# Spreading a weight conversion over more steps, and putting off three blocks instead of two

## The chip, the core and the metric

The kernel runs on one core of one Trainium2 chip. The metric is device time in microseconds (us): the median of three runs before the change is 971.77 us (971.24 to 972.63). TensorE is PE in the rows (its weight loads PEld), VectorE is DVE, ScalarE is ACT, GpSimd is POOL, and SyncE is SP, which issues every DMA of this kernel.

## What is computed

Three stages follow each other over 4608 tokens of 512 numbers, all in float32:

```
phi(x) = [exp(p - m), exp(-(p - m))],  p = x @ w_phi,  m = max|p|       # 128 + 128 features of each head
attn   = phi(q) @ (phi(k)^T v) / (phi(q) @ sum phi(k) + 1e-6)            # 8 batches, 8 heads, 576 x 64
x      = attn as (4608, 512)
g      = leaky(x @ w_in; alpha)                                          # d_ff = 2048
y      = g @ w_out                                                       # (4608, 512)
logits = y @ phi;  d = softmax over tokens;  c = softmax over 32 slots
s      = d^T @ y;  slot_out[e] = relu(s[e] @ w1[e]) @ w2[e]              # 8 experts, 4 slots each
out    = c @ slot_out
```

`w_in`, `w_out` and `alpha` arrive as 64-bit floats. The kernel never forms `y`: it uses `phi` folded into `w_out` (`wpr`, 2048 x 32) for the logits and gathers `d^T @ g` first.

## The kernel before

**Blocks and steps.** The tokens go in 12 blocks of 384 (`NB`), and each block in 16 chunks of 128 of d_ff (`NC`): 192 steps. A step computes one chunk of `h = x @ w_in` in `gemm` (L513): 12 matrix products of 128x128 by 128x384 into one of two PSUM banks `ph`, since x and w_in are each split in a high and a low part. `leaky` (L525) empties the bank, ACT first (L527), DVE second (L528), into one of five `gT` tiles. A product can start when L528 of the step two before it has run.

**The four chunks of a quad.** `turn_g` (L545) transposes each `gT` on DVE (L547) into a half of a large tile and, after every fourth, adds four products `pl` (L556) to the block's logits. When a block is complete, `softmax` (L565) copies `pl` to `ls` on ACT (L570), forms `pr` on PE (L575), takes its maximum on DVE (L586), the exponential on ACT (L598), transposes it (L608), and `gather` (L616) adds `d^T g` in 48 products of 32x512 over four banks `pS` (L625) if both halves lie in one tile, or 96 of 32x256 if they don't. DVE then adds the four banks to `acc` (L644). `gather` takes both banks of the pool `ps_a` and the pair of `ps_b`.

**Blocks put off.** The tile `gb` that takes the transposes lies where the pool `prep` lay, and `prep` holds what the conversions of the weights need. So blocks 0 to `NDEF`-1 have their `gT` written to DRAM (`gT_d`, L531) and taken up again later, four steps of `QUADS` for a block: `reload` (L533) loads a quad into three double tiles of the ring `vg` (L537) and the tiles `kp1` and `ks` (L543). Their logits `pl` sit in a bank of `ps_a` from the first quad to `ls`; those of the other blocks have a bank of their own. Their halves are `half_of` (L501): `held` in `kall`, which the K pairs use until step 141, and thirds of `gb`.

**Conversion.** `conv` (L183) turns 64-bit words of one chunk of a weight into float32 in six DVE and three ACT instructions (L197 to L209); for `w_out` a transposition (L236), a product with `phi` (L243) and a gather (L249, with the copy L250 on DVE) follow, three steps long. `prep` is closed at step 16 `NDEF`, and the first transposition into `gb` waits for the last of these.

**Beside the steps.** Attention runs for one block ahead: the 32 K pairs (L257 to L381), and per block four `q_pair` (L385) and a `q_finish` (L457), which sends the reciprocal through DRAM (`rc_d`, `bc`), divides (L486) and splits x into `xhi` (ACT, L479) and `xlo` (DVE, L480). From step 158 on, weights of the last stage are fetched (L716, DMA L733), first `w_out` as float32 (`wo`). `combine` (L689) does the softmax over the slots, its largest part behind step 173. All these functions are put into steps by the table at L668 to L709; within the dependences a list scheduler then fixes the order of each engine, and every engine and SP's DMA issue run strictly in that order. Banks and tiles of a pool are given out as the scheduler comes to them.

Of the kernel before, what the change touches and what calls it, by code (L numbers as in the profile page):

```python
# [11 lines left out]
I32 = mybir.dt.int32  # L12
# [22 lines left out]
VT = 5  # L35
KVB = 8
PF = 14
NDEF = 2
QUADS = [[148, 150, 152, 154], [164, 166, 168, 170]]
EARLY = 4  # L40
KPB = 3
QB = 2
# [19 lines left out]
def attention_prelu_softmoe(ctx: ExitStack, tc, qT, kT, v, wphi, w_in, w_out, alpha, phi, w1, w2, out):  # L62
# [9 lines left out]
    wo32 = dram.tile([NC, 128, DM], F32, name="wo32")  # L72
    gT_d = dram.tile([NDEF, NC, 128, BT], F32, name="gT_d")
    rc_d = [dram.tile([2, 32, 2, HB], F32, name=f"rc_d{i}") for i in range(2)]
# [10 lines left out]
    def close_pool(name):  # L85
        pools.pop(name)[0].__exit__(None, None, None)
# [26 lines left out]
    def bank(name, pool=None):  # L113
        if pool is not None:
            return pool.tile([128, 512], F32, tag={id(ps_h): "h", id(ps_l): "l", id(ps_d): "d"}[id(pool)], name=name)
        taken["a"].append([])
        return ps_a.tile([128, 512], F32, tag="a", name=name)
# [59 lines left out]
    def at(slot, phase, fn):  # L177
        at_step(slot, phase, fn)
# [4 lines left out]
    def conv(slot, src, use):  # L183
        st = {}

        def load():
            st["raw"] = prep.tile([128, 1024], I32, tag="raw", name="raw", bufs=3)
            nc.sync.dma_start(st["raw"], src)

        def first():  # L190
            pair = st["raw"].rearrange("p (n t) -> p n t", t=2)
            st["low"], high = pair[:, :, 0].bitcast(U32), pair[:, :, 1].bitcast(F32)
            m = st["m"] = prep.tile([128, 512], F32, tag="m", name="m", bufs=2)
            sign = st["sign"] = prep.tile([128, 512], F32, tag="sign", name="sign", bufs=2)
            rest = st["rest"] = prep.tile([128, 512], F32, tag="rest", name="rest")
            mu, ru = m.bitcast(U32), rest.bitcast(U32)
            nc.scalar.activation(m, high, AF.Abs)  # L197
            nc.scalar.activation(sign, high, AF.Sign)
            nc.vector.tensor_scalar(out=m, in0=m, scalar1=F64_LEAST, scalar2=F64_MOST, op0=ALU.max, op1=ALU.min)
            nc.vector.tensor_scalar(out=mu, in0=mu, scalar1=3, scalar2=0x40000000, op0=ALU.logical_shift_left, op1=ALU.bitwise_xor)  # L200
            nc.vector.tensor_scalar(out=ru, in0=mu, scalar1=0x7F800000, scalar2=None, op0=ALU.bitwise_and)
            nc.vector.scalar_tensor_tensor(out=rest, in0=st["low"], scalar=2.0 ** -52, in1=rest, op0=ALU.mult, op1=ALU.mult)  # L202
            nc.scalar.activation(m, m, AF.Abs)

        def second():
            m = st["m"]
            nc.vector.tensor_tensor(out=m, in0=m, in1=st["rest"], op=ALU.add)  # L207
            w = prep.tile([128, 512], F32, tag="w32", name="w32", bufs=2)
            mark[slot + 1] = nc.vector.tensor_tensor(out=w, in0=m, in1=st["sign"], op=ALU.mult).ins  # L209
            use(slot, w)  # L210

        at(slot - 2, "pre", load)
        at(slot, "pre", first)
        at(slot + 1, "pre", second)
# [12 lines left out]
    def use_w_out(c):  # L227
        def use(slot, w):
            st = {}
            for i in range(4):  # L230
                nc.sync.dma_start(wo32[4 * i + c // 4, 32 * (c % 4):32 * (c % 4) + 32, :], w[32 * i:32 * i + 32])

            def trans():
                pt = bank("pwt")
                for k in range(KD):
                    nc.tensor.transpose(pt[:, 128 * k:128 * k + 128], w[:, 128 * k:128 * k + 128], ident)  # L236
                st["wT"] = prep.tile([128, 512], F32, tag="wT", name="wT")
                nc.scalar.copy(st["wT"], pt)

            def product():  # L240
                pw = bank("pw", ps_l)
                for k in range(KD):
                    nc.tensor.matmul(pw[32 * k:32 * k + 32, 0:128], phi_sb[:, k, :], st["wT"][:, 128 * k:128 * k + 128], start=True, stop=True)  # L243
                st["sw"] = prep.tile([128, 128], F32, tag="sw", name="sw")
                nc.scalar.copy(st["sw"], pw[:, 0:128])

            def gather():
                pw = bank("pw2", ps_l)
                nc.tensor.matmul(pw[:, 0:32], st["sw"], tident[:, 0:32], start=True, stop=True)  # L249
                nc.vector.tensor_copy(wpr[:, c, :], pw[:, 0:32])  # L250

            at(slot + 2, "pe", trans)
            at(slot + 3, "pe", product)
            at(slot + 4, "pe", gather)
        return use
# [241 lines left out]
    pl_t, pl_read, gT_t = {}, {}, {}  # L497
    odd_turn = {n: n % 2 for n in range(NDEF, NB)}
    held = kall[:, 0:6144].rearrange("p (h c t) -> p h c t", h=2, c=8)

    def half_of(n, h):  # L501
        if n == 0 or (n < NDEF and h):
            return held[:, h]
        return gbt[0][:, 1 if h else 2 if n < NDEF else 2 * odd_turn[n]]

    def turned(n):
        if n == 0:
            return [(held, slice(0, 2))]
        if n < NDEF:
            return [(gbt[0], slice(2, 3)), (held, slice(1, 2))]  # L510
        return [(gbt[0], slice(2, 0, -1) if odd_turn[n] else slice(0, 2))]

    def gemm(n, c):  # L513
        xhi, xlo = xhi_t[n], xlo_t[n]
        ph = ps_h.tile([128, 512], F32, tag="h", name="ph")
        h = ph[:, 0:BT]
        first = [(k, a, b) for k in range(KD) for a, b in ((0, 0), (1, 0))] + [(k, 0, 1) for k in range(KD)]
        terms = first if c == 0 else [(k, a, b) for k in range(KD) for a, b in ((0, 0), (0, 1), (1, 0))]
        for i, (k, a, b) in enumerate(terms):
            gemm_last[0] = nc.tensor.matmul(  # L520
                h, (w_in_hi, w_in_lo)[a][c][:, 128 * k:128 * k + 128], (xhi, xlo)[b][:, k, :],
                start=(i == 0), stop=(i == len(terms) - 1)).ins
        return h

    def leaky(n, c, h):  # L525
# [3 lines left out]
        mark[NC * n + c] = ins  # L529
        if n < NDEF:  # L530
            nc.sync.dma_start(gT_d[n, c], gT)  # L531
# [145 lines left out]
        q_finish(-39 + 18 + 5 if n == 0 else NC * (n - 1) + 7, n)  # L677
    for c in range(NC):
        conv(int(-16 + 1.25 * c), w_in[c].bitcast(I32), use_w_in)
        conv(int(10 + 1.25 * c), w_out[c].bitcast(I32), use_w_out(c))  # L680
    for n in range(NDEF, NB):
        softmax(NC * (n + 1) + 1, n)
    for m, slots in enumerate(QUADS):
        for quad, slot in enumerate(slots):
# [51 lines left out]
    gbt, views = [], []  # L736
# [11 lines left out]
    for step in range(-45, nslots + 4):  # L748
        slot = real.get(step)
        for fn in sched.get((step, "pre"), ()):  # L750
            fn()
        h = None
        if slot is not None:
            n, c = divmod(slot, NC)
            if 0 <= slot < nslots:
                h = gemm(n, c)
            pn, pc = divmod(slot - 1, NC)
            if NDEF <= pn < NB:
                turn_g(pn, pc)
        for fn in sched.get((step, "pe"), []) + sched.get((step, "pe2"), []):  # L760
            fn()
        if h is not None:
            leaky(n, c, h)
        for fn in sched.get((step, "post"), ()):
            fn()
        if slot is None:
            continue
        if slot == NC * NDEF:
            close_pool("prep")
            gbt.append(open_pool("gp").tile([128, 3, 8, BT], F32, tag="gb", name="gb"))  # L770
        if slot == QUADS[0][-1] + 4:
            fetch_k(0, 6)
        if slot == QUADS[1][-1] + 4:
            fetch_k(6, 16)
            fetch(attk, "kp1")
            fetch(attk, "ks")
        if slot == 168:
            close_pool("attq")
            pf = open_pool("pf", "right")
            for i in range(2):  # L780
                fetch(pf, f"hr{i}", 2)
            for i in range(PF - 4):
                fetch(pf, f"pf{i}")
        if slot == NC * (NB - 1):
            fetch(xp, "num", 3)
            fetch(xp, "bc", 3)
        if NC * (NB - 1) < slot <= nslots:
            fetch(wring, f"w{(slot - 1) % NC}", 2)
        if slot == 181:
            fetch_half(0)  # L790
        if slot == nslots:
            fetch(xp, "xhi", 3)
            fetch(xp, "xlo", 3)
# [174 lines left out]
```

## Time and profile before

| | us |
|---|---|
| median of three runs | 971.77 |
| profiled execution, its own time | 973.75 |
| its span, first to last instruction | 971.9 |
| PE busy | 928.3 |
| DVE busy | 722.1 |
| ACT busy | 443.6 |

The profiled execution is 1.85 us longer than its span and 1.98 us longer than the median. Shares over the whole span hide that the stages differ: in the first quarter DVE is nearly always busy, in the middle PE has no idle time at all, and in the last 30 us the DMA engines write the output.

### The profile page before, as it was taken

Reading aid. Unit: us, or ns where it says so; the run is one execution under the profiler, and the core shown is the slowest. Engines: PE = TensorE matmul, PEld = TensorE weight load, DVE = VectorE, ACT = ScalarE, POOL = GpSimd, SP = SyncE. Lnnn points to the kernel's source line nnn. Section 1 sums busy time; section 2 is a strip of 40 time slices with the busy share of each in tenths; the row PEclk is TensorE's granted clock in tenths of the full one; section 3 lists DMA queues with packets and bytes.
Section 4 is the critical chain, followed back from the end, with each engine's and each line's share of the span. In section 5 each row is a group of like instructions: output and inputs, shape, how many; then the busy total and the mean of one; then the engine's idle time right before and its main releaser. Section 6 shows DMA issues by size and latency. Waiting matters only on the chain.

```text
span 971.9 us, 20072 instructions
## 1 busy us (share of the span) xinstructions
PE 928.3 (96%) x8178; PEld 654.1 (67%) x8178; DVE 722.1 (74%) x1425; ACT 443.6 (46%) x867; POOL 143.5 (15%) x84
## 2 busy tenths in 40 slices
PE   6888989999989999999999999999999999899997
PEld 3446676777668676676677776776777667786454
DVE  6998999989686687677677778677756767864233
ACT  5876757766635345245335344353342341221113
POOL 4102212112112112122022112121130220000000
PEclk9898999999999999999999999999999999999999
DMA  7345655674231031031211210200212609478999
GB/s 272 119 141 177 207 169 196 213 203 122 64 87 28 23 85 43 26 78 53 51 44 42 59 53 25 75 26 23 54 34 72 177 1 302 159 268 260 311 354 335
DMA packets 75675, 122.22 MB, mean 126 GB/s; under 512 B 7872, under 2 KB 49472, under 8 KB 75584
## 3 DMA queue, kind: packets, MB, share of 16 engines
q1 hardware_dynamic: 75584, 120.95, 40.3%
q8 instruction: 64, 1.05, 0.5%
q14 instruction: 27, 0.22, 0.1%
HBM read 99.82 MB, written 21.10 MB: 124 GB/s over the span
## 4 chain that ended last, share of the span: by engine, by line
PE 74%; DVE 17%; DMA 4%; issue 2%; ACT 2%; SPq 0%; DVEq 0%; ACTq 0%
PE ph L520 37%; PE num L440 5%; PE pkv L336 5%; PE pS L625 4%; PE pl L556 4%; PE pq L407 3%; PE den L445 3%; PE pk L293 2%; PE pso L866 2%; DVE m L207 2%; DVE gT L528 1%; PE pe L846 1%; DVE mx L281 1%; PE po L902 1%; DVE rest L202 1%
## 5 line engine op out<-in xcount | busy, mean ns | idle before, releaser
L520 PE MATMUL ph<-xhi,w 128*128 128x384 f32 x1536 | 430.8, 351 | 8.2 <-ACT xhi L479 4.0
L520 PEld LDWEIGHTS ph<-xhi,w 128*128 128x128 f32 x1536 | 280.3, 189 | 71.5 <-issue 38.0
L520 PE MATMUL ph<-xlo,w 128*128 128x384 f32 x768 | 257.9, 341 | 0.9 <-DVE xlo L480 0.8
L419 POOL PARTITION_ALL_REDUCE mb<-pj x48 | 137.4, 2864 | 477.4 <-ACT pj L413 326.8
L527 ACT ACTIVATE gT<-ph 128x384 f32<-128x384 f32 x192 | 93.3, 488 | 245.3 <-PE ph L520 239.9
L528 DVE SCALAR_TENSOR_TENSOR gT<-gT,alpha_rest,ph 128x384 f32<-128x384 f32 x192 | 115.7, 604 | 103.8 <-ACT gT L527 102.4
L520 PEld LDWEIGHTS ph<-xlo,w 128*128 128x128 f32 x768 | 144.4, 189 | 9.7 <-issue 4.8
L547 DVE STREAM_TRANSPOSE gb<-gT 128x384 f32<-128x384 f32 x162 | 92.0, 571 | 2.9
L429 ACT ACTIVATE qe<-pj 128x768 f32<-128x768 f32 x90 | 72.2, 839 | 22.9 <-DVE pj L423 14.0
L440 PE MATMUL num<-qe,kv 128*64 128x192 f32 (+1 forms) x488 | 68.6, 411 | 3.5 <-ACT qe L429 3.3
L336 PE MATMUL pkv<-kall 128*64 128x256 f32 x464 | 57.9, 393 | 1.3 <-ACT kall L287 0.7
L281 DVE TENSOR_REDUCE mx<-pk 128x4 f32<-128x512 f32 (+1 forms) x80 | 49.5, 623 | 7.2 <-PE pk L293 5.8
L407 PE MATMUL pq<-qraw,wp 64*128 64x384 f32 x192 | 46.8, 545 | 7.9 <-DMA qraw<-in_qT_dram 4.1
L286 ACT ACTIVATE kall<-kall 128x512 f32<-128x512 f32 x60 | 37.5, 627 | 30.4 <-DVE kall L283 30.2
L440 PEld LDWEIGHTS num<-qe,kv 128*64 128x64 f32 x488 | 31.1, 136 | 27.8 <-issue 18.0
L324 DVE TENSOR_TENSOR ks<-ks,kall 128x256 f32<-128x256 f32 x96 | 47.4, 517 | 0.4
L336 PEld LDWEIGHTS pkv<-kall 128*64 128x64 f32 x464 | 31.6, 140 | 23.5 <-issue 4.8
L423 DVE TENSOR_TENSOR pj<-pj,mb 128x768 f32<-128x768 f32 x48 | 44.8, 932 | 0.0
L283 DVE TENSOR_TENSOR kall<-pk,mx 128x512 f32<-128x512 f32 x60 | 40.8, 680 | 2.2 <-PE pkv L336 1.7
L293 PE MATMUL pk<-wp,kall 64*128 64x128 f32 x512 | 39.5, 293 | 2.9 <-issue 2.6
L293 PEld LDWEIGHTS pk<-wp,kall 64*128 64x128 f32 x512 | 32.9, 194 | 12.8 <-issue 10.8
L413 ACT COPY pj<-pq 128x768 f32<-128x768 f32 x44 | 35.0, 796 | 13.4 <-PE pq L407 13.2
(203 smaller groups left out, 1157.6 us busy)
## 6 DMA issues: line engine op xcount, KB each, us to landing
w<-in_w_dram SPq DMA_DIRECT2D x46, 256.0 KB
kall<-in_v_dram SPq DMA_DIRECT2D x30, 320.0 KB
qraw<-in_qT_dram SPq DMA_DIRECT2D x48, 192.0 KB
bc<-rc_d SPq DMA_DIRECT2D x24, 384.0 KB
out_dram<-os SPq DMA_DIRECT2D x18, 512.0 KB
raw<-in_w_in_dram SPq DMA_DIRECT2D x16, 512.0 KB
raw<-in_w_out_dram SPq DMA_DIRECT2D x16, 512.0 KB
gT_d<-gT SPq DMA_DIRECT2D x32, 192.0 KB
```

The lines of the kernel that those rows point to most:

```text
L281: nc.vector.tensor_reduce(out=mx[:, 0:nt], in_=src, axis=AX.X, op=ALU.max, apply_absolute_value=True)
L293: lambda t=t, j=j, sl=slice(64 * j, 64 * j + 64): nc.tensor.matmul(st["pk"][:, j, F * t:F * t + F], st["kraw"][sl, 128 * t:128 * t + 128], ...
L324: nc.vector.tensor_tensor(out=ks[:, j], in0=ks[:, j], in1=f[t], op=ALU.add)
L336: return lambda: nc.tensor.matmul(pkv[64 * j:64 * j + 64, 0:256], st["vt"][:, t, 64 * j:64 * j + 64], part.rearrange("p s f -> p (s f)"), ...
L407: lambda j=j, sl=slice(64 * j, 64 * j + 64): nc.tensor.matmul(pq[j][:, 0:BT], wp[sl, F * j:F * j + F], st["qraw"][sl], start=True, stop=True)
L419: nc.gpsimd.partition_all_reduce(mb, pj, 128, bass_isa.ReduceOp.absmax)
L429: nc.scalar.activation(st["e", s], pj, AF.Exp, scale=(1.0, -1.0)[s])
L440: lambda s=s, j=j: nc.tensor.matmul(num[64 * j:64 * j + 64, o:o + w], kvs[:, s, 64 * j:64 * j + 64], st["e", s][:, j, o:o + w], start=(s = ...
L520: gemm_last[0] = nc.tensor.matmul(h, (w_in_hi, w_in_lo)[a][c][:, 128 * k:128 * k + 128], (xhi, xlo)[b][:, k, :], start=(i == 0), stop=(i = ...
L527: nc.scalar.activation(gT, h, AF.Relu, scale=-1.0)
L528: ins = nc.vector.scalar_tensor_tensor(out=gT, in0=gT, scalar=alpha_rest[:, c:c + 1], in1=h, op0=ALU.mult, op1=ALU.add).ins
L547: nc.vector.transpose(out=half_of(n, c // 8)[:, c % 8, :], in_=gT)
```

## The change

`NDEF` goes from 2 to 3, so that block 2 too is written to DRAM and `prep` stays open until step 48. The conversions of `w_out` start at steps 10 + 2.2 c (10 to 43) instead of 10 + 1.25 c (10 to 28). The blocks put off are taken up in three groups, at steps 146 to 152, 156 to 162 and 166 to 172, instead of two at 148 to 154 and 164 to 170. Block 1 now has both halves in `held`; blocks 0 and 2 have one in `held` and one in `gb`, so the gathers of two blocks instead of one take 96 products. The first fetch of `wo` into `held` moves from step 158 to 166, the second from 174 to 176.

```diff
-NDEF = 2
-QUADS = [[148, 150, 152, 154], [164, 166, 168, 170]]
+NDEF = 3
+QUADS = [[146, 148, 150, 152], [156, 158, 160, 162], [166, 168, 170, 172]]
...
     def half_of(n, h):
-        if n == 0 or (n < NDEF and h):
+        if n == 1:
             return held[:, h]
-        return gbt[0][:, 1 if h else 2 if n < NDEF else 2 * odd_turn[n]]
+        if n < NDEF:
+            return gbt[0][:, n] if h else held[:, n // 2]
+        return gbt[0][:, 1 if h else 2 * odd_turn[n]]
 
     def turned(n):
-        if n == 0:
+        if n == 1:
             return [(held, slice(0, 2))]
         if n < NDEF:
-            return [(gbt[0], slice(2, 3)), (held, slice(1, 2))]
+            return [(held, slice(n // 2, n // 2 + 1)), (gbt[0], slice(n, n + 1))]
...
-        conv(int(10 + 1.25 * c), w_out[c].bitcast(I32), use_w_out(c))
+        conv(int(10 + 2.2 * c), w_out[c].bitcast(I32), use_w_out(c))
...
-        if slot == QUADS[0][-1] + 4:
+        if slot == QUADS[1][-1] + 4:
             fetch_k(0, 6)
-        if slot == QUADS[1][-1] + 4:
+        if slot == QUADS[2][-1] + 4:
             fetch_k(6, 16)
```

Lines from L503 on have numbers two higher after the change (L520 is L522, L625 is L627).

**First place: PE, at the last chunk of `w_out`.** `pw` is the gather of a chunk, `pkv`, `den` and `num` are attention, `w_850` is chunk 7 of block 2 before, `w_615` chunk 0 of block 3 after. Before:

```order
L445 MATMUL den<-qe,zt 32x192 x4
L249 MATMUL pw_2892<-tident,sw 128x32
L336 MATMUL pkv<-kall 64x256 x8
L336 MATMUL pkv<-kp,kall 64x256 x2
L556 MATMUL pl<-gT,wpr 32x384 x4
L342 MATMUL pkv<-ks,ones 32x128 x4
L520 MATMUL ph<-xhi,w_850 128x384
```

After:

```order
L522 MATMUL ph<-xhi,w_1226 128x384
L293 MATMUL pk<-wp,kall 128x128 x8
L249 MATMUL pw_3439<-tident,sw 128x32
L440 MATMUL num<-qe,kv 64x192 x8
L522 MATMUL ph<-xhi,w_615 128x384 x6
L445 MATMUL den<-qe,zt 32x192 x8
```

Before, 36 rows of attention and conversion stand between the products of steps 38 and 39, and the last gather of `w_out` is among them; now that gather stands between the products of steps 47 and 48, which follow each other.

**Second place: PE, the last block put off.** `pr` belongs to block 1 before and to block 2 now, `pS` is its gather; `w_1061` and `w_1226` are steps 172 and 175, `w_615` is step 176. Before:

```order
L575 MATMUL pr<-ls,tident 128x384
L520 MATMUL ph<-xhi,w_1024 128x384
...
L520 MATMUL ph<-xhi,w_1061 128x384
L625 MATMUL pS<-gb,d 32x256 x48
L625 MATMUL pS<-kall,d 32x256 x48
L556 MATMUL pl<-gT,wpr 32x384 x4
```

After:

```order
L522 MATMUL ph<-xhi,w_1226 128x384
L577 MATMUL pr<-ls,tident 128x384
L627 MATMUL pS<-kall,d 32x256 x48
L627 MATMUL pS<-gb,d 32x256 x48
L522 MATMUL ph<-xhi,w_615 128x384 x8
```

Before, the products of steps 171 and 172 stand between `pr` and its gather; now nothing does.

**Third place: DVE, the same stretch after the change,** from the leaky step 173 (first row) to that of step 174 (last row):

```order
L530 SCALAR_TENSOR_TENSOR gT<-gT,alpha_rest,ph 128x384
L486 TENSOR_TENSOR num<-bc,num 128x384 x4
L549 STREAM_TRANSPOSE gb<-gT_8505 128x384
L480 TENSOR_TENSOR xlo<-num,xhi 128x384
L588 TENSOR_REDUCE mbl<-pr 128x1
L610 STREAM_TRANSPOSE d<-dT 128x384
...
L695 TENSOR_REDUCE cm<-logits 128x28
L696 TENSOR_TENSOR logits<-logits,cm 128x896
L698 TENSOR_REDUCE cm<-logits 128x28
L704 TENSOR_TENSOR cw<-logits,cm 128x512
L530 SCALAR_TENSOR_TENSOR gT<-gT,alpha_rest,ph 128x384
```

The division, transpositions of the block put off (`gT_8505` is one that was reloaded), its softmax and the whole first part of `combine` now stand between two leaky steps; before, three leaky steps (171 to 173) stood between the maximum of `pr` and the division, and the division came behind `combine`, not ahead of it.

## Rows read from the trace of the kernel before

**Rows 1.** The page, parts 1 and 2: busy us, share; tenths per fortieth.

```profile
PE 928.3 (96%) x8178; PEld 654.1 (67%) x8178; DVE 722.1 (74%) x1425; ACT 443.6 (46%) x867; POOL 143.5 (15%) x84
...
PE   6888989999989999999999999999999999899997
...
DVE  6998999989686687677677778677756767864233
```

**Rows 2.** Windows: from:to, length, busy us (count) by engine, PE clock, DMA, GB/s.

```profile
145.00:285.00 140.00, 134.58 (x1087) 98.23 (x1085) 124.88 (x253) 89.53 (x177) 22.35 (x12) 0.99 0.51 153
185.00:205.00 20.00, 19.94 (x151) 15.60 (x150) 17.48 (x38) 14.38 (x30) 0.21 (x1) 1.00 0.68 212
205.00:225.00 20.00, 19.57 (x163) 15.19 (x161) 18.90 (x41) 13.34 (x28) 2.74 (x1) 1.00 0.71 201
276.00:279.50 3.50, 3.50 (x16) 3.44 (x13) 2.08 (x5) 1.74 (x3) 0.00 (x0) 0.55 0.18 44
815.00:820.00 5.00, 5.00 (x37) 3.68 (x36) 4.92 (x11) 1.46 (x3) 0.00 (x0) 1.00 1.05 387
```

**Rows 3.** Timeline of PE: start, us, line, count, and the wait ahead of it.

```profile
275.54 0.56 PE L342 MATMUL pkv<-ks,ones 128*32 128x128 f32 x8 [2.44 <-DVE ks L328]
...
797.71 3.41 PE L625 MATMUL pS<-gb,d 32*32 32x512 f32 x96
...
813.19 0.84 PE L556 MATMUL pl<-kall,wpr 128*32 128x384 f32 x4 [0.22 <-DMA kall<-gT_d]
...
829.05 1.90 PE L625 MATMUL pS<-gb,d 32*32 32x256 f32 x83
...
832.92 1.38 PE L625 MATMUL pS<-kall,d 32*32 32x256 f32 x52 [0.66 <-issue]
834.24 0.85 PE L556 MATMUL pl<-gT,wpr 128*32 128x384 f32 x8
...
843.40 1.63 PE L520 MATMUL ph<-xhi,w 128*128 128x384 f32 x8 [1.63 <-DVE gT L528]
```

**Rows 4.** Timeline of DVE, around the gathers of blocks 0 and 9.

```profile
746.85 1.04 DVE L547 STREAM_TRANSPOSE kall<-kall 128x384 f32<-128x384 f32 x2 [3.08 <-DMA kall<-gT_d]
...
801.11 2.72 DVE L644 SCALAR_TENSOR_TENSOR acc<-acc,sc,pS 128x512 f32<-128x512 f32 x4 [0.50 <-PE pS L625]
803.75 2.87 DVE L547 STREAM_TRANSPOSE gb<-kall 128x384 f32<-128x384 f32 x6
806.54 1.00 DVE L547 STREAM_TRANSPOSE gb<-gT 128x384 f32<-128x384 f32 x2
807.46 0.58 DVE L528 SCALAR_TENSOR_TENSOR gT<-gT,alpha_rest,ph 128x384 f32<-128x384 f32 x1
```

**Rows 5.** Timeline of ACT: the logits of block 0 copied from their bank.

```profile
757.63 0.48 ACT L570 COPY ls<-pl 128x384 f32<-128x384 f32 x1 [1.83 <-DMA rc_d<-rd]
```

**Rows 6.** The chain that ended last, 825 to 862 us: start, us, what.

```profile
825.40 0.47 DVE mbl L586
...
827.25 0.58 DVE d L608
...
829.55 1.00 DVE cm L693
...
831.53 1.01 DVE logits L694
...
832.56 0.96 ACT logits L695
...
833.54 1.10 DVE cm L696
...
839.34 1.88 DVE num L486 x4
...
843.26 1.41 DVE xlo L480 x3
...
860.32 8.54 PE ph L520 x48
```

## The prediction, written before the changed kernel ran

> **What bounds the kernel now.** I read the page first. PE is busy 96% of the span and DVE 74%, and the fortieths show where DVE is not slack: the first quarter, where its digits are 9 and 8 while PE's vary, and a few slices late [rows 1]. So the time of PE's work is fixed, and the change can only move the idle time of PE, its clock, and the number of its products. Second come the windows by stage. From 145 to 285 us, where the conversions of `w_out` run, PE is busy 134.58 of 140.00 us, so 5.42 us of idle time is there, with DVE at 124.88 of 140.00, or 89% [rows 2]. [...] Last, the timelines of PE, DVE and ACT and the chain of waits over the blocks put off, 745 to 862 us [rows 3 to 6]; there the chain runs through DVE's `mbl`, `d`, `combine`, the division and `xlo` in a row, from 825 to 844, and only then through 48 products [rows 6].
>
> The profiled execution took 973.75 us. I add up in its time and take off 1.98 at the end, its distance from the median of 971.77.
>
> **The early part: what is removed.** The first place of the order shows the stop of the products between steps 38 and 39, with 36 rows of attention and conversion in it, gone: the last conversion now ends between steps 47 and 48. No conversion is added or taken away, only spread over 34 steps for 19. What can be won is the idle time, 5.42, and the slow clock, (1 - 0.55) x 3.50 = 1.57 us: 7.0 in all [rows 2]. What remains: DVE has the same work in the stretch as a whole, 89% of it. Where it was at 17.48 of 20 (87%) PE idled 0.06, and where it was at 18.90 (95%) it idled 0.43 [rows 2]. Seven such stretches at some 0.2 make 1.5. So I take 7.0 - 1.5 = **-5.5**. The bounds are -7.0 (nothing remains) and -2.5 (only the one long wait of 2.44 goes, and the short ones are spread with the conversions). The chunks of block 2 are now written to DRAM; in 145 to 285 the DMA share is 0.51 [rows 2], and I cost these 16 writes at nothing, since nobody waits for them for over 500 us; the 16 transpositions that they put off, 7.7 us at 0.48 [rows 4], are in the late part below. Some of them stood in this stretch, which would make DVE's 89% smaller; I take nothing more off for it.
>
> **The late part: what is added.** From step 64 to 146 PE's order is the same before and after, and I take the middle at no change. Then come four terms.
>
> 1. A second gather of 96 products. The one of before runs from 829.05 to the next product at 834.24, 5.19 us with a pause of 0.66 in it; the form of 48, which the profile counts as x96, took 3.41 us at 797.71 [rows 3]. **+1.8**; 1.1 if the pause does not come back.
> 2. Three starts that are late in steps 150 to 161. The second group starts 8 steps ahead of where it did, and lies on the gathers of blocks 0 and 8. The copy `ls` of block 0 shares ACT with a DMA that it had to wait for, 1.83 us at 757.63 [rows 5]; I take 0.5 of it as seen by PE. The product of step 156 waits for the leaky step 154, which stands on DVE behind four adds (2.72), ten transpositions (2.87 for six, 1.00 for two, and two more at 1.00) and its own 0.58 [rows 4], 8.2 us in all, after a gather that ends 3.2 us into the same stretch: 11.4 against PE's 10.6, or 0.8. A similar, smaller one at step 161, 0.3. **+1.6**, between 0 (PE has that work ready to pull ahead) and 3 (all of 1.83, and 1.2 more).
> 3. The last group, where the second place of the order shows nothing between `pr` of block 2 and its gather, and step 176 right behind that. Step 176 needs the leaky step 174; the third place shows what DVE does before that. From the end of block 1's gather: four adds 2.72; eight transpositions 3.87 and, further on, eleven at 0.48, 5.3; four leaky steps 2.32 [rows 4]; the division 1.88 and four `xlo` at 0.47, 1.88; `mbl` 0.47 and some 0.4 of small ones behind it; `d` 0.58; three small transpositions of `pr`, estimated at a third of a microsecond each, 1.0; `combine` with 1.00, 1.01, ACT's 0.96, 1.10 and `cw`, which I estimate at the 1.0 of an instruction of that size, with 0.3 of small ones: 5.4 [rows 6]. Sum 25.8. The quads of block 2 must also have arrived: DVE waited 3.08 us for such a reload at 746.85 [rows 4]; here it has other work first, and I put it at 2.0. So 27.8. PE in the same time: five products of a step at 8.54 / 4 = 2.13 [rows 6], 10.7; `num` some 1.4; five groups of `pl` at 0.84 [rows 3], 4.2; `pr` 0.6; the gather 5.19. Sum 22.1. DVE is longer by **+5.7**. If the reload does not hold it, 3.7; if it lands 4 us later than I think, 9.7.
> 4. The clock. PE then idles some 4 us between `pr` and the gather. Behind the 2.44 us wait of before, the clock was at 0.55 for 3.5 us [rows 2, 3]. The gather is run at that clock too, but DVE is the longer in that time, so only what is left of the slow stretch behind the gather shows: **+0.5**, between 0 and 1.6.
>
> Against these goes what disappears: PE's waits at 813.19 (0.22) and 843.40 (1.63) [rows 3], which belong to the group that was taken up at steps 164 to 170: **-1.85**. The fetches of `wo` into `held` are 8 steps later. In the old place nobody waits on them for 40 us, so I cost that at nothing by itself; what it does to the reload is a rival.
>
> Sum: -5.5 + 1.8 + 1.6 + 5.7 + 0.5 - 1.85 = +2.25, so 976.0 in the time of the profiled execution and **974.0** as a median, 0.23% above before. What a measurement of this kernel can tell from no change is about 0.2%, or 1.94 us, so "same" is 969.8 to 973.7.
>
> **Rivals.**
>
> *The reload is early and DVE has slack: not slower.* The point from which it decides is when DVE comes to the first reloaded transposition of block 2, about 11 us behind the end of block 1's gather by the list above. If the quads are there by then, the last group costs 3.7, not 5.7, and the hole before the gather is too short to move the clock (0.5 goes). With the early gain at 6.5: -6.5 + 1.8 + 0.8 + 3.7 - 1.85 = -2.05, a median of 969.7; with the early gain as forecast, 970.7. For it: the last two quads are eight tiles of 128 x 384 words, 1.57 MB, or 4.1 us at the 387 GB/s of 815 to 820 [rows 2]. Against: the same reload made DVE wait at 746.85, with nothing else in the queues [rows 4]. A further step on this side is that the list order lets PE take all of the late holes (terms 2 and 4 zero, term 3 at 2): 968.
>
> *The reload is behind `wo`: slower still.* On SP, the second half of block 2's reload stands behind seven issues for `wo` of 128 x 512 words, 1.84 MB. In the window 815 to 820 the DMA share is 1.05 at 387 GB/s [rows 2], so these bytes take 1.84 MB / 387 GB/s = 4.7 us, and if the reload waits for them, the 2.0 us of term 3 become 6.7: a median of 978.7. Against it: DVE reaches these quads only some 11 us behind the end of block 1's gather, which is also what lets the fetch of `wo` start, so 4.7 us of bytes may be through by then. [...]
>
> *The clock.* If the slow stretch starts with the hole and lasts through gather and step 176, as 0.55 did over 3.5 us [rows 2], all of 1.6 is seen: 975.1. [...]
>
> *The change does not do what it says.* The conversions are spread, but DVE stays full because the attention work, which PE was ahead with, is pulled into the gaps, and only the 2.44 us wait goes. Early part -2.5: a median of 977.0. For it: DVE had 18.90 of 20 with hardly a gap already from 205 to 225 [rows 2], far from the last conversion.
>
> **How the numbers follow.** My forecast with its own bounds (972.3 to 976) 0.40; early reload 0.23, with all late holes filled 0.08; reload behind `wo` 0.12; the clock 0.07; no early relief 0.10. Slower by over 0.2% are three fifths of the forecast, 0.24, and nearly all of the last three, 0.27: 0.51. Faster are the last rival of the other side, 0.08, and over half of the early reload, 0.14: 0.22. The rest, 0.27, is the same. The two unlikely ends (early part -7.0 with a late part near nothing, and a reload 4 us late without early relief) are left out: 968.0 to 978.7.
>
> **What would show it.** The early part is right if no wait of PE over 1 us stands between 245 and 290, step 48's product follows step 47's, the clock is 1.00 there, and PE's idle time up to 285 has fallen by about 4; it is wrong if the idle time is spread out but still above 4. The last group is right if PE waits 3 to 5 us ahead of the 96 products that follow `pr` of block 2, at about 835 to 850, with DVE without a gap over 1 us but for one of about 2 us on `gT_d`; it is wrong if DVE idles there, or if PE has no wait over 2 us. Term 2 is right if waits on L530 of 0.5 to 1 us stand ahead of steps 156 and 161. The sum is wrong altogether if the middle, 330 to 745, changes by more than 1 us, since there I counted nothing.

## The result, and the profile after

The changed kernel took 982.22 us (median of 4, 979.69 to 983.10) against 971.58 us for the kernel before on the same chip: a ratio of 1.0102, 95% interval 1.0087 to 1.0116. The forecast was 974.0 in a range of 968.0 to 978.7: the sign was right, the size was not, and the time lies outside the range. The profiled execution took 979.69 us, with a span of 977.9.

The page's shares say little: PE 96% and DVE 74%, as before. The windows of PE do, here of the changed kernel (columns as in [rows 2]):

```profile
145.00:285.00 140.00, 138.79 (x1097) 103.97 (x1095) 123.21 (x246) 91.37 (x179) 24.15 (x12) 1.00 0.55 168
745.00:800.00 55.00, 54.30 (x519) 37.71 (x520) 44.70 (x89) 21.25 (x41) 11.28 (x4) 1.00 0.29 94
836.00:840.00 4.00, 1.40 (x7) 0.78 (x5) 3.66 (x11) 2.24 (x6) 0.00 (x0) 1.00 1.05 386
840.00:845.00 5.00, 2.84 (x98) 2.08 (x100) 4.06 (x8) 0.99 (x4) 0.00 (x0) 0.68 1.05 387
845.00:850.00 5.00, 3.01 (x122) 1.56 (x94) 4.62 (x9) 1.11 (x3) 0.00 (x0) 0.84 1.04 377
850.00:855.00 5.00, 5.00 (x38) 3.96 (x26) 4.89 (x9) 0.97 (x2) 0.00 (x0) 0.80 0.75 270
```

The early part did what was expected: 1.21 us of idle time are left of the 5.42 in 145 to 285 [rows 2], and the clock there is 1.00. The loss is late, in a stretch of 20 us. Two engines are needed to read it. PE's timeline (start, us, and in brackets the wait ahead):

```profile
829.93 0.84 PE L558 MATMUL pl<-kall,wpr 128*32 128x384 f32 x4 [2.49 <-DMA kall<-gT_d]
...
836.59 0.81 PE L577 MATMUL pr<-ls,tident 128*128 128x384 f32 x2
842.16 3.01 PE L627 MATMUL pS<-kall,d 32*32 32x256 f32 x82 [4.76 <-DVE logits L614]
...
848.24 2.00 PE L627 MATMUL pS<-gb,d 32*32 32x256 f32 x62 [1.99 <-issue]
850.17 2.51 PE L522 MATMUL ph<-xhi,w 128*128 128x384 f32 x8
```

and DVE's, over the same stretch:

```profile
816.87 2.72 DVE L646 SCALAR_TENSOR_TENSOR acc<-acc,sc,pS 128x512 f32<-128x512 f32 x4 [0.70 <-PE pS L627]
...
829.91 1.04 DVE L549 STREAM_TRANSPOSE gb<-kall 128x384 f32<-128x384 f32 x2 [4.39 <-DMA kall<-gT_d]
...
833.20 1.96 DVE L486 TENSOR_TENSOR num<-bc,num 128x384 f32<-128x384 f32 x4
...
837.81 0.55 DVE L588 TENSOR_REDUCE mbl<-pr 128x1 f32<-128x384 f32 x1
...
841.71 0.30 DVE L614 STREAM_TRANSPOSE logits<-pr 32x128 f32<-32x128 f32 x1
842.04 1.09 DVE L695 TENSOR_REDUCE cm<-logits 128x28 f32<-128x896 f32 x1
...
846.97 1.16 DVE L704 TENSOR_TENSOR cw<-logits,cm 128x512 f32<-128x512 f32 x2
848.05 0.61 DVE L530 SCALAR_TENSOR_TENSOR gT<-gT,alpha_rest,ph 128x384 f32<-128x384 f32 x1
```

What to see: both engines stand still until the reload of block 2 is there at 829.9; then DVE has work until 842 with no gap over 0.31 us, PE only until 837.4, and PE cannot start step 176 in the 4.76 us, because the leaky step 174, which it needs, stands behind `combine` at 848.05. The gather then has a pause of 1.99, and the clock is 0.68, 0.84 and 0.80 from 840 to 855.

The timeline of SP's queue tells why the reload is late: seven fetches of `wo` are issued ahead of it, and its own first issue comes at 824.42. The last line, of SP's waits from 822 to 828 (us in total, times, longest), tells what that issue waited for:

```profile
819.55 2.97 SPq L735 DMA_DIRECT2D kall<-wo  x6
822.69 0.33 SPq L735 DMA_DIRECT2D hr<-wo  x1
824.42 0.89 SPq L539 DMA_DIRECT2D kall<-gT_d  x2
825.52 0.33 SPq L545 DMA_DIRECT2D gT<-gT_d  x1
826.19 0.36 SPq L539 DMA_DIRECT2D kall<-gT_d  x1
826.87 0.33 SPq L545 DMA_DIRECT2D gT<-gT_d  x1
```

```profile
SPq L539 <- DMA bc<-rc_d: 1.3, 1, 1.3
```

The profile puts that wait down to an older transfer, the reciprocals of attention (`bc`), here and in comb_late; in the second trace of the changed kernel it names a leaky step. From its first issue at 824.42 to the first transposition that uses it at 829.91 the reload then took 5.5 us.

The start of ACT's part of a step, one instruction for each of the 192 steps in either trace, gives the account:

| step | before | after | after - before |
|---|---|---|---|
| 146 | 728.98 | 717.72 | -11.26 |
| 173 | 837.41 | 827.47 | -9.94 |
| 176 | 846.13 | 853.43 | +7.30 |
| 191 | 885.48 | 892.64 | +7.16 |
| end of the span | 971.9 | 977.9 | +6.0 |

By step 146 the changed kernel has not yet done block 2's logits, `pr` and gather, some 7.4 us of PE's work by estimate (four groups of 0.84 and a gather of 3.41 [rows 3], and 0.6 for `pr`); so the early gain is 11.26 - 7.4 = 3.9 us. Late, 7.4 is paid back, and with it PE's waits of 2.49 + 4.76 + 1.99 = 9.24 where before had 0.66 + 1.63 + 0.22 = 2.51 [rows 3]; 0.70 of idle time in 745 to 800, where there was none; the clock, 0.32 x 2.84 + 0.16 x 3.01 + 0.20 x 5.00 = 2.4 us; and 0.5 us for the longer form of block 2's gather (3.94, measured in comb_late below, for 3.41). That is 7.4 + 6.7 + 0.7 + 2.4 + 0.5 = 17.7 of the 11.26 + 7.30 = 18.6 us by which steps 146 to 176 are longer; 0.9 us stays without an account.

### The profile page after: what moved, and what is told of

It is laid out like the page before. It is cut to its first block, busy times and chain, and to the rows that moved or that the text cites. A ratio compares the mean times of both kernels' runs of the same rounds, so it can differ in the third digit from the quotient of the medians.

```text
span 977.9 us, 20338 instructions
## 1 busy us (share of the span) xinstructions
PE 936.8 (96%) x8274; PEld 658.1 (67%) x8274; DVE 719.6 (74%) x1425; ACT 444.5 (45%) x867; POOL 147.7 (15%) x84
## 4 chain that ended last, share of the span: by engine, by line
PE 74%; DVE 15%; DMA 4%; ACT 4%; issue 2%; SPq 0%; DVEq 0%; ACTq 0%
PE ph L522 37%; PE num L440 5%; PE pkv L336 5%; PE pS L627 4%; PE pl L558 4%; PE den L445 3%; PE pq L407 3%; PE pk L293 2%; PE pso L868 2%; PE pe L848 1%; DVE m L207 1%; PE po L904 1%; DVE gT L530 1%; DVE rest L202 1%; DMA bc<-rc_d 1%
## 5 line engine op out<-in xcount | busy, mean ns | idle before, releaser
L522 PE MATMUL ph<-xhi,w 128*128 128x384 f32 x1536 | 433.3, 351 | 6.1 <-ACT xhi L479 3.7
L522 PEld LDWEIGHTS ph<-xhi,w 128*128 128x128 f32 x1536 | 279.8, 189 | 70.9 <-issue 38.9
L522 PE MATMUL ph<-xlo,w 128*128 128x384 f32 x768 | 256.9, 340 | 0.1
L419 POOL PARTITION_ALL_REDUCE mb<-pj x48 | 141.6, 2950 | 498.6 <-ACT pj L413 400.8
L530 DVE SCALAR_TENSOR_TENSOR gT<-gT,alpha_rest,ph 128x384 f32<-128x384 f32 x192 | 116.4, 607 | 117.0 <-ACT gT L529 116.1
L522 PEld LDWEIGHTS ph<-xlo,w 128*128 128x128 f32 x768 | 144.0, 188 | 8.0 <-issue 5.1
L549 DVE STREAM_TRANSPOSE gb<-gT 128x384 f32<-128x384 f32 x148 | 84.5, 573 | 2.9
L407 PE MATMUL pq<-qraw,wp 64*128 64x384 f32 x192 | 50.2, 567 | 4.8 <-DMA qraw<-in_qT_dram 3.8
L627 PE MATMUL pS<-gb,d 32*32 32x512 f32 (+1 forms) x1056 | 40.3, 569 | 2.1 <-issue 2.0
L293 PEld LDWEIGHTS pk<-wp,kall 64*128 64x128 f32 x512 | 34.5, 200 | 11.4 <-issue 7.3
```

Of the source, the lines that this page charges most:

```text
L293: lambda t=t, j=j, sl=slice(64 * j, 64 * j + 64): nc.tensor.matmul(st["pk"][:, j, F * t:F * t + F], st["kraw"][sl, 128 * t:128 * t + 128], ...
L407: lambda j=j, sl=slice(64 * j, 64 * j + 64): nc.tensor.matmul(pq[j][:, 0:BT], wp[sl, F * j:F * j + F], st["qraw"][sl], start=True, stop=True)
L419: nc.gpsimd.partition_all_reduce(mb, pj, 128, bass_isa.ReduceOp.absmax)
L522: gemm_last[0] = nc.tensor.matmul(h, (w_in_hi, w_in_lo)[a][c][:, 128 * k:128 * k + 128], (xhi, xlo)[b][:, k, :], start=(i == 0), stop=(i = ...
L530: ins = nc.vector.scalar_tensor_tensor(out=gT, in0=gT, scalar=alpha_rest[:, c:c + 1], in1=h, op0=ALU.mult, op1=ALU.add).ins
L549: nc.vector.transpose(out=half_of(n, c // 8)[:, c % 8, :], in_=gT)
```

## The experiments

Theory A: what starts the loss is block 2's reload, which waits for the fetch of `wo` issued ahead of it. Theory B: DVE's list in the last group is too long in any case. Theory C: a large part is the clock behind the waits. Each result is the median, then its ratio to runs of the kernel before that were made together with it, and the 95% interval of that ratio.

**The changed kernel again (after_again).** No edit.

> The changed kernel once more, unchanged: a second trace beside the first. Its first profiled execution took 979.69 us, at a granted clock of 0.990, and three others 981.7 to 983.1 at 0.981. Theory A (the late stretch starts with block 2's reload that waits for the fetch of wo) and theory B (DVE's list alone is too long) both expect the same waits: PE about 2.5 us on gT_d, 4.8 us ahead of the gather of block 2, and about 2 us within it. If the 2 to 3 us between executions are the clock, a trace of a slower one shows a window of clock under 0.9 that the first did not have, most likely behind one of these waits; if they are waits, one of the three is longer.

Measured: 981.77 us, 1.0088 (1.0072 to 1.0104). Its profiled execution took 977.42: the same three waits of PE, 2.17, 4.76 and 1.50 us. Theories A and B both expected them, so this run doesn't decide between the two; and as its trace is of the quickest execution, it doesn't tell where the slower ones spend their time.

**The reload ahead of `wo` (reload_first).**

```diff
-        if slot == QUADS[1][-1] + 4:
-            fetch_k(0, 6)
...
         if slot == 168:
+            fetch_k(0, 6)
             close_pool("attq")
...
-            nc.sync.dma_start(t, src)
+            ins = nc.sync.dma_start(t, src).ins
+            if len(got) < 7:
+                tc.add_manual_dep(ins, reloaded[0].name, nosync, reason="reload first")
```

`reloaded` holds the last DMA of `reload`; the dependence adds an order on SP and no wait. PE's and DVE's orders stay as they were.

> Only the order on SP changes: the second half of block 2's reload is issued ahead of the six fetches of wo into kall, not behind them (one fetch of wo, 0.26 MB, stays ahead). Theory A: DVE's wait of 4.39 us on gT_d falls to 1 us or less, PE's 2.49 us there goes, and what follows on DVE is 3 to 4 us earlier; 4 us faster than the changed kernel, about 978. Theory B: DVE waits less, but its list up to the leaky step 174 is the longer anyway, so PE's wait ahead of the gather grows by what the other loses; under 1 us gained. If the transfers share the bandwidth evenly whatever the order of issue, the wait on gT_d stays above 3 us.

Measured: 977.75 us, 1.0055 (1.0042 to 1.0068), 4.0 us faster than the changed kernel. DVE's wait for the first of these tiles, of its timeline:

```profile
826.92 1.04 DVE L551 STREAM_TRANSPOSE gb<-kall 128x384 f32<-128x384 f32 x2 [0.95 <-DMA kall<-gT_d]
```

and all of PE's waits between 820 and 860 (us in total, times, longest):

```profile
PE pS L629 <- DVE logits L616: 4.8, 1, 4.8
PE pS L629 <- issue: 1.8, 1, 1.8
```

SP's timeline around the same reload:

```profile
823.28 0.89 SPq L541 DMA_DIRECT2D kall<-gT_d  x2
...
825.71 4.64 SPq L737 DMA_DIRECT2D kall<-wo  x6
```

Theory A holds for this part: the order of issue alone takes 4.39 to 0.95 on DVE and PE's wait on `gT_d` to nothing. The reload is issued 1.1 us earlier than in the changed kernel, and from its first issue to the first transposition it takes 826.92 - 823.28 = 3.6 us for the 5.5 there. Theory B holds for the rest: the 4.76 us ahead of the gather is there to the hundredth, with the reload late or in time, so the lists of PE and DVE decide it.

**`combine` later (comb_late).**

```diff
-    at(NC * (NB - 1) - 3, "post", lambda: combine(0, NT - 8))
+    at(NC * (NB - 1) + 4, "post", lambda: combine(0, NT - 8))
```

> The larger part of combine moves from step 173 to step 180, with the reload left behind wo; the scheduler then puts the products of steps 176 and 177 between pr of block 2 and its gather. Theory A: the wait of 2.5 us on gT_d stays and most of the 4.8 us too, since what is late is the reload; 1 to 2 us gained. Theory B: PE's wait ahead of the gather falls to under 1 us, 4 to 6 us gained, about 977.

Measured: 974.71 us, 1.0018 (1.0007 to 1.0030), 7.1 us faster than the changed kernel and more than either theory gave. PE's waits between 820 and 860:

```profile
PE pl L558 <- DMA kall<-gT_d: 3.2, 1, 3.2
```

Its gather of block 2, and the window around it:

```profile
847.24 1.91 PE L627 MATMUL pS<-kall,d 32*32 32x256 f32 x82
...
849.00 2.25 PE L627 MATMUL pS<-gb,d 32*32 32x256 f32 x93
851.18 0.44 PE L522 MATMUL ph<-xhi,w 128*128 128x384 f32 x1
```

```profile
846.00:852.00 6.00, 6.00 (x205) 4.66 (x204) 5.40 (x11) 1.44 (x2) 0.00 (x0) 1.00 1.01 324
```

The wait on the reload is still there, as theory A says; the 4.76 is gone, as theory B says, since steps 176 and 177 now stand in it. With it go the pause and the slow clock: the gather takes 851.18 - 847.24 = 3.94 us for the 8.01 of the changed kernel.

**Both edits (reload_comb).**

> Both edits, the reload ahead of wo and combine at step 180. Theory A and B each hold for a part: 7 to 9 us gained, about 974, with PE's waits from 820 to 850 under 2 us in sum. If it gains no more than the better of the two alone, both edits relieve the same wait.

Measured: 970.40 us, 0.9976 (0.9966 to 0.9986), 11.4 us faster than the changed kernel where the two alone gave 4.0 + 7.1 = 11.1. PE's waits between 820 and 860 and the window of the old hole:

```profile
PE ph L522 <- DVE xlo L480: 0.2, 1, 0.2
```

```profile
826.00:846.00 20.00, 19.75 (x278) 13.68 (x278) 18.17 (x41) 6.78 (x15) 0.00 (x0) 1.00 1.05 377
```

The two edits take away different waits, and together they account for the whole loss. This version also beats the kernel before, by 0.24%.

**The changed kernel a third time (after_third).** No edit.

> The changed kernel a third time, for its trace alone. Both traces so far are of its quicker executions (979.69 and 977.42 us, clock 0.989 to 0.990), and nine others took 981.3 to 983.1 at 0.981 to 0.985. If this trace is of such a one, the 3 to 4 us are seen in it: theory C expects the granted clock under 0.9 over a longer stretch behind the waits of 820 to 850 than the 10 to 15 us of the first trace; theory A and B, which know waits only, expect longer waits. If it is a quick one again, this stays open.

Measured: 980.27 us. (The executions that the expectation counts as nine were eight.) PE's waits are 2.98, 4.76 and 1.50. Windows of this trace:

```profile
830.00:835.00 5.00, 4.12 (x16) 3.50 (x16) 4.14 (x9) 0.00 (x0) 0.00 (x0) 0.71 1.06 379
...
845.00:850.00 5.00, 4.18 (x130) 2.54 (x99) 3.85 (x6) 1.33 (x2) 0.00 (x0) 0.58 1.04 372
```

Here the clock fell behind the first wait too (0.71 in 830 to 835), and was 0.58 in the gather. The loss by clock is 0.29 x 4.12 + 0.42 x 4.18 = 3.0 us in these two windows alone, against 2.4 in all in the first trace. The three waits add up to 9.24 us in either trace, so the 0.6 us between these two executions fits theory C; the 2 to 3 us of the slower ones are not shown by it, since no trace is of an execution over 981 us.

**Empty queues (quiet).** The reload is issued first, and all later fetches for the last stage wait for block 2's gather:

```diff
+            if len(got) < 50:
+                tc.add_manual_dep(ins, gathered[0].name, full_dep, reason="after the gather")
```

The fetches of steps 166 to 177 are moved behind step 176 for this (not shown).

> The reload ahead of all fetches, and no fetch for the last stage issued before the gather of block 2 has ended, so that the DMA queues are nearly empty in PE's wait ahead of it. It tells what the pause of 1.5 to 2.0 us within that gather is. If it comes from queues that are full (386 GB/s there in the changed kernel) it is gone or under 0.7 us, as in the kernel before, where they were light; if it comes from the long wait ahead of the gather, it stays at 1.5 us or more. Theory A besides: DVE's wait on gT_d falls from 0.95 to near nothing. The last stage gets its weights 20 us later, so the time says little: 976 to 985.

Measured: 982.52 us, 1.0096 (1.0080 to 1.0112); the last stage is the later for its weights, so the time tells nothing here. PE's waits between 830 and 850, and the window of the gather:

```profile
PE pS L629 <- DVE logits L616: 4.8, 1, 4.8
PE ph L522 <- DVE gT L530: 0.3, 1, 0.3
```

```profile
838.00:846.00 8.00, 6.65 (x194) 4.97 (x195) 6.78 (x12) 1.33 (x2) 0.00 (x0) 0.60 0.02 4
```

With 4 GB/s in the queues the pause is gone, behind the same 4.76 us; the slow clock is not (0.60). So behind this wait the pause was there with full queues (381 GB/s in the changed kernel, 372 in reload_first) and not with empty ones, and the slow clock was there with both. Full queues were not enough for it: with both edits they moved 377 GB/s, and block 2's gather ran through. DVE's wait for the reload did not fall to nothing but came in two pieces, 1.44 and 0.36.

The traces tell more of the pause than its name, "issue". Counted along PE's instructions (products, weight loads and its semaphore instructions together), it stands ahead of number 14,274 in all four traces that have it in block 2's gather. Other gathers of 96 products have a short one, with 5 GB/s in the queues and no wait ahead: block 1's in the kernel before ahead of number 14,018, and block 0's in eight traces of the changed kernel and its variants ahead of number 12,738 (12,739 in narrow_conv), here with both edits:

```profile
761.60 0.66 PE L629 MATMUL pS<-gb,d 32*32 32x256 f32 x14 [0.46 <-issue]
```

These places lie whole multiples of 256 instructions apart. The table sets beside the pause how long PE had taken for the 256 instructions up to the place (in us):

| gather | GB/s | 256 instructions, without the pause | pause |
|---|---|---|---|
| block 1, kernel before | 5 | 3.14 | 0.66 |
| block 0, both edits | 5 | 3.07 | 0.46 |
| block 2, quiet | 4 | 3.85 | none |
| block 2, changed kernel, first trace | 381 | 4.08 | 1.99 |
| block 2, reload_first | 372 | 4.04 | 1.78 |
| block 2, both edits | 386 | 7.88 | none |

With the pause, 256 instructions take 5.8 to 6.1 us in all four cases with full queues, and 3.3 to 3.8 with light ones. Behind the 4.76 us the gather ran through its 256 instructions in 4.08 and 4.04 us and then paused; with both edits, where steps 176 and 177 fill that stretch with longer products, they took 7.88 us and no pause came. The trace counts transfers of a queue called "instruction": one in 838 to 850 of the changed kernel, which has the pause, and two in 838 to 846 of quiet, which has none. What PE waits for in the pause is not shown, and no run changed it by itself.

**The conversions as before (narrow_conv).** On top of both edits:

```diff
-        conv(int(10 + 2.2 * c), w_out[c].bitcast(I32), use_w_out(c))
+        conv(int(10 + 1.25 * c), w_out[c].bitcast(I32), use_w_out(c))
```

> Reload first and combine late, but the conversions of w_out at steps 10 to 28 as before the change: the part of the gain that comes from spreading them. Three blocks put off and prep open until step 48 remain. If the early gain comes from the spread, about 4 us are lost against the 970.4 us of the kernel with both edits, and PE's idle time from 145 to 285 us is 4 us or more. If it comes from prep staying open, so that nothing waits for the last conversion, it is lost for 1 us or less.

Measured: 971.79 us, 0.9997 (0.9986 to 1.0008). The window of the conversions:

```profile
145.00:285.00 140.00, 138.13 (x1094) 103.16 (x1092) 117.96 (x238) 89.34 (x178) 21.07 (x11) 1.00 0.53 161
```

Neither reading holds alone: the idle time is 1.87 us, not 4, and between 0.9976 and 0.9997 lie about 2 us, not 4 and not under 1; the two intervals just touch. The larger part of the idle time goes with `prep` open until step 48, whether the conversions are spread or not; of the time, by the ratios, 2 us of the early 4 go with the spread, and from step 16 to 146 this trace is 2.6 us longer than those with the spread.

**The kernel before with `combine` later (before_comb, pair_two), beside the repaired one (pair_three).** The edit of comb_late alone on the kernel before, first on its own, then on one chip with the kernel with both edits.

> The kernel before the change, with the larger part of combine at step 180 in place of 173 and nothing else. In its trace DVE's list around 825 to 844 cost PE one wait of 1.63 us and one of 0.66. Theory B (combine in the way of a block put off is what costs) expects 1 to 2.5 us gained, 970 to 971.5, so that part of what the two edits gave is not owed to the third block. Theory A expects no more than 1 us.

> The changed kernel with both edits (reload first, combine at step 180) again, now on one chip with the kernel of before with its combine at step 180. If three blocks and the spread are worth the 4 us that the steps up to 64 show, less the second long gather and the starts of steps 150 to 161, this one is 1 to 3 us the faster of the two; if what the repaired kernel gains over the kernel before is owed to combine alone, they agree within 0.7 us.

> The kernel before with its combine at step 180, the other half of the pair: about 970.6 us; see there.

Measured: before_comb 970.63 us, 0.9977 (0.9966 to 0.9987), 2.4 us gained, as theory B expected. PE's wait of 1.63 us [rows 3] is gone from its trace; one of 0.6 on `xhi` is left. On one chip: with three blocks and both edits 969.51, 0.9968 (0.9956 to 0.9980); the kernel before with the later `combine` 970.22, 0.9978 (0.9967 to 0.9989). The two differ by 0.7 us with intervals that overlap. So of the 3.1 us by which the repaired kernel beats the kernel before in this pair, 2.4 are there with the later `combine` alone, which needs no third block. Three blocks and the spread bring no gain that these runs can tell.

## Why the prediction was wrong

Direction and place were right, and of the chain the part from DVE's list to PE's wait ahead of the gather; the size was not: +10.6 us measured, +2.25 forecast. The step that failed is the one that has block 2's reload hold DVE for only 2.0 us, and PE not at all. Step by step, by the terms of the sum:

- **Early part, -5.5: somewhat too large.** It measured -3.9 here, and over eight traces with the spread -9.7 to -12.1 at step 146 less the 7.4 us moved, so -2.3 to -4.7. The idle time fell by 4.2 as I said it would show. The scatter stands ahead of step 16, which I had not looked at: from step 16 to 146 all eight took 554.3 to 554.4 us for the 565.0 to 566.5 of three traces with the order of before, 10.7 to 12.1 less, so 3.3 to 4.7 without the work moved. Whether steps 0 to 16 became slower isn't shown: they took 77.9 to 80.7 us, and 77.9 to 78.6 in those three. The middle held (steps 80 to 146, 280.8 us in both), though PE's order from step 64 on was not quite the same: attention products had moved behind it, and steps 64 to 80 took 3.7 us longer.
- **Term 1, the long gather, +1.8: mis-sized.** Without pause or slow clock the long form costs 3.94 for 3.41, 0.5 us. Its pause of 0.66 was a given number to me; it came back as 1.99 with queues at 381 GB/s.
- **Term 2, late starts in steps 150 to 161, +1.6: too large.** 0.70 us of idle time in 745 to 800; the longest wait on L530 there was 0.3.
- **Term 3, the last group, +5.7: the step that failed first.** I put the reload at 2.0 us of DVE's wait; it was 4.39, 4.07 and 4.88 in three traces and, in comb_late, 5.09, and what I gave as the rival "the reload is behind `wo`", with a chance of 0.12, is what happened, though with 2.4 us more of DVE's wait than the 2.0, not the 4.7 more that I had priced. I had argued that the bytes of `wo` would be through when DVE got there, some 11 us behind block 1's gather. DVE got there at 825.5, 8.6 us behind it, since the first reloaded transpositions stand ahead of the division in its list; SP's rows show the reload issued only from 824.42. I also let DVE's wait only lengthen DVE's list; PE waited for the same tiles, 2.49 us. Waits of 7.25 for 5.7.
- **Term 4, the clock, +0.5: mis-sized.** 2.4 us in the first trace, 3.0 in two windows of the third. I took it as hidden behind DVE, but it stretched the gather and the two steps behind it. Behind the one wait of 4.76 us the granted clock was 0.50 to 0.84 in the three traces.
- **The step from the trace to the median, -1.98: wrong by itself.** I took off what the profiled execution of before had over its median. But that is one execution's place in a scatter: the kernel before took 968.23 to 976.34 us in later runs, with medians of 972.60 to 972.99. The changed kernel's three profiled executions took 977.42 to 980.27 and its eight others 981.34 to 983.10, so here the sign is the other way round: 982.22 - 979.69 = +2.5. Of the 8.2 us by which 974.0 was missed 4.5 lie here, and 3.7 in the sum itself (+5.94 in the profiled times for +2.25). The others ran at a mean clock of 0.981 to 0.985, and reload_first and comb_late, which each lack a part of the stall, show no clear step (profiled and median 977.27 and 977.75; 974.03 and 974.71). But with both edits, where neither stall is left, the profiled execution lay 1.8 us below its median too (968.60 and 970.40). So a longer slow stretch behind the two waits is only argued: no trace is of such an execution, and it stays open.

The rival of the other side fell at its deciding point: the quads were not there when DVE came to them. The one of "no early relief" fell too, since 1.21 us of idle time are left of 5.42; but the pair shows the early gain nearly spent again even when both stalls are removed. From step 146 to 180 the kernel with both edits took 135.1 and 135.7 us in its two traces, the kernel before with the later `combine` 125.2 in both of its: 7.4 of that is the work moved, and 2.5 to 3.1 is spent late. It is not idle time, of which PE has 1.15 and 1.34 us from 745 to 860 in the one and 1.15 and 1.18 in the other; the longer gather is 0.5 of it, and the rest stays open.

## What to carry to other kernels

Work that was put off came back here where the queues (386 GB/s) and the vector engine (no gap over 0.31 us from 830 to 842) had their own rush: before moving it, list by engine and by DMA queue what stands there, and look at what is issued ahead of the transfer that the next product needs. The block that one late transfer released was late on both engines at once (4.39 us on DVE, 2.49 on PE); and as DVE's list was the longer, PE waited for it a second time, whether the transfer was late or not (4.76 us in either case). Taking the work that isn't needed yet (here `combine`) out of that list was worth more than the transfer, 7.1 us for 4.0. And try the same repair on the old kernel before giving its gain to the change.

## What the runs showed of the hardware

PE paused in the middle of gathers of 96 small products without a releaser in the profile ("issue"): 1.5 to 2.0 us when the DMA engines were full (348 to 386 GB/s over the four gathers), 0.2 to 0.7 us when they moved 5 GB/s. In every trace that has such a pause it stands at places in PE's instruction stream that are whole multiples of 256 instructions apart (one instruction off in narrow_conv), and the 256 ahead of it had been run in 4.6 us or less. The fastest stretch of 256 up to such a place, with its pause, took 5.8 us under full queues and 3.3 under light ones. What PE waited for there is not shown.

The granted clock fell behind one wait of 4.76 us with the queues full (0.68, then 0.84, in the changed kernel) and with them empty (0.60 in quiet), and behind a wait of 2.98 us in one execution of the changed kernel (0.71 in after_third), but not behind 2.17 and 2.49 us at the same place in two others (1.00); in the kernel before 2.44 us had left it at 0.55 [rows 2].

And the place of one profiled execution against the median of the others did not carry over from the kernel before to the changed one: 2.2 us above it before the change, 2.5 below after, with runs of the kernel before that spread over 8 us.
